# A spectral filter and a gated feed-forward on one core: another order of the opening stage

## Chip, cores and metric

One NeuronCore of a Trainium2 chip. The metric is the device time of one execution in microseconds (us). Engines: TensorE (PE; weight loads are shown as PEld), VectorE (DVE), ScalarE (ACT), GpSimd (POOL) and SyncE, whose queue (SP) issues all transfers of this kernel.

## What is computed

```python
x = A_x                                    # (1, 2048, 640) bf16
xn = layernorm(x)                          # over the 640, eps 1e-5
s = irfft2(rfft2(xn) * (w_r + 1j * w_i))   # over both axes, in fp32, rounded to bf16
g = silu((gelu(xn @ w_gate) * (xn @ w_up)) @ w_down)   # 640 -> 1536 -> 640
return x + s * g
```

## The kernel before

**Tiles.** The 2048 rows are 16 slabs of 128 rows (slab n1 holds the rows n1, n1 + 16, ...). X holds all of them, 640 columns each, and is normalised in place. The feed-forward works on four groups of four slabs, that is 512 rows, as columns of xnT[g] (640 as 5 x 128 partitions, by 512). The 1536 hidden features are 12 tiles t of 128. A piece `ffn_piece(g, t, k, c0, c1)` (lines 782 to 795) is five matmuls over the 5 x 128 of the contraction, with the gate weights (k = 0, PSUM tag psg, evicted by a gelu on ACT to `ge`) or the up weights (k = 1, PSUM tag psu, multiplied by `ge` on DVE into `uT`). Each of the two PSUM tags has two buffers, `ge` has three. The spectral part is done by matmuls with sine tables, which are made on chip from constants of one column (`fwd_consts`, `inv_consts`, `inv_rest`, `ft_v`, lines 283 to 355), and stands between the pieces of the feed-forward later on.

**Order.** The schedule is written by hand: each engine runs its instructions in the order in which the program issues them, and waits in that order. `back` (line 854) is the list of TensorE's steps, `plan[s]` what other work is put behind step s by `put`. Steps 0 to 2 work on slabs 0 and 1 with tiles t = 0, 1, 2, 128 columns at a time (`ffn_slab`). Then come `ffn_part(0, t, 0)` for t = 3 to 7, with 256 columns (slabs 0 and 1), then the second half, `ffn_part(0, t, 1)` for t = 0 to 7 (slabs 2 and 3), and then whole groups of 512 columns.

**The opening.** SP issues the loads in the order of lines 95 to 109: x of slab 0, gate tiles 0 to 2, x of slab 1, up tile 0, up tiles 1 and 2, x of slabs 2 and 3, and the other weights. Per slab, `stats` is two BATCH_NORM_STATS2 of 320 columns and one aggregate on DVE, `root` adds eps on DVE and raises to -0.5 on POOL, `norm` subtracts and multiplies on DVE, and TensorE transposes (`slab_Tparts` in two parts of three and two blocks for slabs 0 and 1, `slab_T` in one for slabs 2 and 3), with a copy out of PSUM. Until slab 0 is there, TensorE runs matmuls on a tile of ones (`warm_pe`, 19 and then 2), whose results are not used. ACT loads its gelu table by a small ACTIVATE at line 215. `root(0, 1)` (line 321) is followed on DVE by the nine operations of `inv_consts`; `root(1, 1)` (line 979) by the five of `inv_rest`. Then, after the last lines below, the loop over `back` runs.

Of the kernel before, what the change touches and what calls it, by code (L numbers as in the profile page):

```python
# [12 lines left out]
ACT = mybir.ActivationFunctionType  # L13
# [19 lines left out]
def kernel(  # L33
# [40 lines left out]
    with tc.manual_schedule():  # L74
        build(nc, locals())


def build(nc, env):
# [5 lines left out]
    def load_x(n0, n, eng=nc.sync):  # L84
        eng.dma_start(out=X[:, n0:n0 + n, :], in_=xv[:, n0:n0 + n, :])

    def load_w(k, t0, t1):
        f0, f1 = t0 * P, t1 * P
        nc.sync.dma_start(out=(Wg, Wu)[k][:, :, f0:f1], in_=(wgv, wuv)[k][:, :, f0:f1])

    def load_gu(t0, t1):
        for k in range(2):
            load_w(k, t0, t1)

    load_x(0, 1)
    load_w(0, 0, 3)
    load_x(1, 1)
    load_w(1, 0, 1)
    load_w(1, 1, 3)
    load_x(2, 2)  # L100
    load_gu(3, 5)
    load_gu(5, 7)
# [63 lines left out]
    def c1(name, dt=FP32):  # L166
        return consts.tile([P, 1], dt, name=name)

    done = set()
    mva = {}  # L170
    rstd = {}
# [7 lines left out]
    def half_stats(n1, k):  # L179
        if k == 0:  # L180
            st_n[n1] = work.tile([P, 2, nc.vector.BN_STATS_DIM], FP32, tag="st", bufs=3, name="st")
        st = st_n[n1]
        nc.vector.bn_stats(out=st[:, k, :], in_=X[:, n1, 320 * k:320 * k + 320])  # L183
        if k == 1:
            g = n1 // 4
            if g not in mva:
                mva[g] = work.tile([P, 4, nc.vector.BN_AGGR_DIM], FP32, tag="mva", bufs=2, name=f"mva{g}")
            nc.vector.bn_aggr(out=mva[g][:, n1 % 4, :], in_=st)

    def stats(n1):  # L190
        for k in range(2):
            half_stats(n1, k)

    def root(n0, n):
        m = mva[n0 // 4][:, n0 % 4:n0 % 4 + n, :]
        ve = work.tile([P, 4], FP32, tag="ve", name="ve")[:, 0:n]
        nc.vector.tensor_scalar(out=ve, in0=m[:, :, 1], scalar1=1e-5, scalar2=None, op0=ALU.add)  # L197
        r = work.tile([P, 4], FP32, tag="rst", bufs=4, name="rst")[:, 0:n]
        nc.gpsimd.tensor_tensor(out=r, in0=ve, in1=mhalf[:, 0:n], op=ALU.pow)  # L199
        rall[n0] = r  # L200
        for k in range(n):
            rstd[n0 + k] = r[:, k:k + 1]

    def norm(n1, c0=0, c1_=D):
        nc.vector.tensor_scalar(out=X[:, n1, c0:c1_], in0=X[:, n1, c0:c1_], scalar1=mva[n1 // 4][:, n1 % 4, 0:1],  # L205
                                scalar2=rstd[n1], op0=ALU.subtract, op1=ALU.mult)
        if c1_ == D:
            done.add(("n", n1))
# [3 lines left out]
    negpi = c1("negpi")  # L212
    nc.vector.memset(negpi, -PI_SAFE)
    warm = c1("warm")
    nc.scalar.activation(out=warm, in_=negpi, func=ACT.Gelu_apprx_tanh)
    b_0, b_1 = c1("b_0"), c1("b_1")
    nc.vector.memset(b_0, 320.0)
    nc.vector.memset(b_1, 0.0)
# [34 lines left out]
    def affine(name, src, a, b):  # L253
        t = c1(name)
        nc.vector.tensor_scalar(out=t, in0=src, scalar1=float(a), scalar2=float(b), op0=ALU.mult, op1=ALU.add)
        return t
# [7 lines left out]
    def fma(name, src, k, add, dt=FP32):  # L264
        t = c1(name, dt)
        nc.vector.scalar_tensor_tensor(out=t, in0=src, scalar=float(k), in1=add, op0=ALU.mult, op1=ALU.add)
        return t
# [8 lines left out]
    def times(name, src, k, by):  # L276
        t = c1(name)
        nc.vector.scalar_tensor_tensor(out=t, in0=src, scalar=k, in1=by, op0=ALU.mult, op1=ALU.mult)
        return t
# [18 lines left out]
    def inv_consts():  # L298
        i_0 = affine("i_0", pf, 4.0, 0.0)
        i_1 = affine("i_1", pf, 4.0, 4.0)  # L300
        i_2 = affine("i_2", pf, 4.0, 2.0)
        o_0 = affine("o_0", pf, 2.0, 320.0)
        o_1 = affine("o_1", pf, 2.0, 2.0)
        o_2 = affine("o_2", pf, 2.0, 321.0)
        o_3 = affine("o_3", pf, 2.0, 1.0)
        ab.extend([(i_0, o_0), (i_1, o_1), (i_2, o_2), (i_2, o_3)])
        kc.append(affine("l_s", s_f, 2.0, 256.0))
        kc.append(affine("hk", h_f, -2.0, 1.0))

    def inv_rest():  # L310
        cq, l_s, hk = kc
        l_k = fma("l_k", h_f, 2.0, l_s)
        l_r = fma("l_r", times("lh", hk, 1.0, hi_f), 1.0, l_k)
        i_r = affine("i_r", l_r, 2.0, 0.0)
        o_r = fma("o_r", l_r, 1.0, cq)
        ab.append((i_r, o_r))
# [1 line left out]
    fwd_consts()  # L318
    vt_iota(0)
    stats(0)  # L320
    root(0, 1)
    inv_consts()

    def tinv_phase(h):
        sl = slice(8 * h, 8 * h + 8)
# [260 lines left out]
    def warm_pe(n):  # L586
        if not warm_bank:
            warm_bank.append(bank(0))
        for _ in range(n):
            nc.tensor.matmul(warm_bank[0][:, 0:256], lhsT=ones[:, 0:P], rhs=ones, start=True, stop=True)  # L590
# [180 lines left out]
    def bank(k):  # L771
        return psA.tile([P, 512], FP32, tag="gu"[k], name="ps" + "gu"[k])
# [55 lines left out]
        for t, k in tk:  # L828
            ffn_piece(0, t, k, j * P, j * P + P)

    GG, REST = ((0, 0), (1, 0)), ((0, 1), (2, 0))

    def run(*items):
        for it in items:
# [2 lines left out]
    PARTS = ((0, 3), (3, 5))  # L837

    def norm_parts(n1):
        for a, b in PARTS:  # L840
            norm(n1, a * P, b * P)

    def slab_Tparts(n1):
        if n1 == 0:
            xnT[0] = xg.tile([P, 5, 512], BF16, tag="xg", name="xnT0")
        for (a, b), ev in zip(PARTS, (nc.scalar.copy, nc.scalar.copy if n1 == 0 else nc.vector.tensor_copy)):
            pt = psB.tile([P, 5, P], BF16, tag="b")
            for c in range(a, b):
                nc.tensor.transpose(out=pt[:, c, :], in_=X[:, n1, c * P:(c + 1) * P], identity=ident)
            ev(out=xnT[0][:, a:b, n1 * P:n1 * P + P], in_=pt[:, a:b, :])  # L850
        done.add(("T", n1))

    NP = 8
    back = [(run, (ffn_slab, 0, GG), (norm_parts, 1), (vt_iota, 1), (ffn_slab, 0, REST), (slab_Tparts, 1),
             (ffn_slab, 0, ((1, 1), (2, 1))),
             (half_stats, 2, 0)),
            (run, (ffn_slab, 1, GG + REST[:1]), (half_stats, 2, 1), (root, 2, 1), (ffn_slab, 1, REST[1:])),
            (run, (ffn_slab, 1, ((1, 1), (2, 1))), (norm, 2), (stats, 3), (root, 3, 1))]
    for h in range(2):
        for t in range(0 if h else 3, NP):  # L860
            back.append((ffn_part, 0, t, h))
# [7 lines left out]
    plan = [[] for _ in back]  # L869

    def put(s, *item):
        plan[s].append(item)

    put(5, norm, 3)
    put(5, slab_T, 2, 1)
    put(6, slab_T, 3, 0)
    for g in range(5):
        put(3 + g, ft_v, g)
        put(8 + g, ft_v, 5 + g)
# [79 lines left out]
    for i, (n0, n) in enumerate(DG):  # L959
        a = vs0 + 7 * i  # L960
# [10 lines left out]
            if (n0 + k) % 2 and 1 < (n0 + k + 3) // 2 < 8:  # L971
                put(min(d + (5 + k if n == 3 else 2), vs0 + 41), load_xt, (n0 + k + 3) // 2)

    warm_pe(19)
    norm_parts(0)
    stats(1)
    slab_Tparts(0)
    warm_pe(2)
    root(1, 1)
    inv_rest()  # L980

    put(5, phase_const)

# [35 lines left out]
```

## Time and profile before

| | |
|---|---|
| median of 3 runs | 201.75 us (201.51 to 202.1) |
| the profiled execution | 201.22 us |
| its span, first to last instruction | 199.4 us |
| TensorE busy | 193.1 us (97%) |
| DVE busy | 131.6 us (66%) |
| ACT busy | 123.1 us (62%) |
| POOL busy | 38.0 us (19%) |
| first matmul that is used (transpose of slab 0) | starts 5.53 us |
| first matmul of the feed-forward | starts 6.59 us |
| second half (slabs 2 and 3) | starts 17.71 us |

Times in the profile are microseconds from the start of the span. A timeline line gives the start, the length, the engine, the source line, the operation, output and inputs with their shapes, how many were merged into the line, and, in brackets, how long the engine had been idle and who released it. Matmuls overlap: the length of a merged line is from the first start to the last end, and five matmuls of 128 columns that take 0.44 us follow the five before them after 0.28 us. Lines on DMA give the size and the time from issue to landing.

### The profile page before, as it was taken

What the parts mean: (1) busy time and instruction counts of PE and PEld (TensorE: products, weight loads), DVE (VectorE), ACT (ScalarE), POOL (GpSimd) and SP (SyncE); (2) the same over time, 40 slices, a digit from 0 to 9 for tenths busy, and PEclk for the clock granted to TensorE, in tenths of its full rate; (3) what the DMA queues carried; (4) which work ended last, traced back from release to release, by engine and by line L of the source; (5) the groups of instructions that cost most, each with busy time, mean ns of one, the idle gap of its engine ahead of it and who ended that gap; (6) DMA issues with size and microseconds to landing.
All of it is one profiled execution on the core that took longest, in us unless ns stands there. A gap on an engine that the chain in (4) does not pass through costs nothing.

```text
span 199.4 us, 4150 instructions
## 1 busy us (share of the span) xinstructions
PE 193.1 (97%) x1534; PEld 118.9 (60%) x1549; DVE 131.6 (66%) x320; ACT 123.1 (62%) x217; POOL 38.0 (19%) x62
## 2 busy tenths in 40 slices
PE   7989999999999999999999999999999999999993
PEld 5778854777555555576633333457765555556772
DVE  7876869999899832223666556423339786878673
ACT  2547657956976677634788687523474747376632
POOL 5427769999030000000000000000000000000000
PEclk9999999999999999999999999999999999999999
DMA  5999999464566647329962022359800416142522
GB/s 176 333 327 337 388 308 186 88 210 173 154 150 158 150 126 278 104 66 298 282 182 98 5 99 102 132 135 292 235 0 35 135 36 194 36 131 46 187 69 66
DMA packets 40325, 32.44 MB, mean 163 GB/s; under 512 B 15088, under 2 KB 38256, under 8 KB 40048
## 3 DMA queue, kind: packets, MB, share of 16 engines
q1 hardware_dynamic: 40304, 32.17, 55.3%
q8 instruction: 12, 0.20, 0.4%
q14 instruction: 9, 0.07, 0.1%
HBM read 19.03 MB, written 7.88 MB: 135 GB/s over the span
## 4 chain that ended last, share of the span: by engine, by line
PE 91%; DVE 4%; DMA 1%; issue 1%; ACT 1%; POOL 1%
PE psu L789 25%; PE psg L789 25%; PE psg L814 13%; PE psu L814 13%; PE pv L706 2%; PE pd L553 2%; PE pu L653 2%; PE pz L543 2%; PE pd L574 2%; PE px L626 2%; DVE st L183 1%; DMA X<-in_A_x_dram 1%; PE pd L557 1%; POOL rst L199 1%; DVE X L205 1%
## 5 line engine op out<-in xcount | busy, mean ns | idle before, releaser
L789 PE MATMUL psu<-xnT,Wu 128*128 128x512 bf16 (+2 forms) x288 | 60.8, 339 | 0.9 <-DVE uT L795 0.3
L789 PE MATMUL psg<-xnT,Wg 128*128 128x512 bf16 (+2 forms) x287 | 60.5, 338 | 0.5 <-issue 0.2
L795 DVE TENSOR_TENSOR uT<-psu,ge 128x512 bf16<-128x512 f32 (+2 forms) x59 | 34.4, 586 | 27.2 <-PE psu L789 21.0
L814 PEld LDWEIGHTS <-uT 128*128 128x128 bf16 x396 | 37.3, 98 | 14.0 <-issue 0.4
L793 ACT ACTIVATE ge<-psg 128x512 bf16<-128x512 f32 (+2 forms) x59 | 30.6, 519 | 22.9 <-PE psg L789 21.1
L789 PEld LDWEIGHTS <-Wu 128*128 128x128 bf16 x295 | 26.9, 98 | 24.7 <-issue 3.2
L789 PEld LDWEIGHTS <-Wg 128*128 128x128 bf16 x295 | 26.6, 98 | 20.6 <-issue 1.6
L814 PE MATMUL psg<-Wd,uT 128*128 128x320 bf16 (+1 forms) x204 | 30.7, 294 | 0.0
L814 PE MATMUL psu<-Wd,uT 128*128 128x320 bf16 (+1 forms) x192 | 28.7, 296 | 0.0
L638 DVE TENSOR_TENSOR X<-xs,W 128x972 bf16<-128x972 bf16 (+2 forms) x22 | 13.3, 648 | 10.2 <-ACT xs L634 9.2
L579 ACT CAST zd<-pd 128x660 bf16<-128x660 f32 x16 | 11.3, 709 | 9.8 <-PE pd L576 6.1
L708 ACT CAST W<-pv 128x640 bf16<-128x640 f32 x16 | 11.1, 696 | 5.0 <-PE pv L706 5.0
L183 DVE BATCH_NORM_STATS2 st<-X 128x6 f32<-128x320 bf16 x32 | 14.0, 477 | 0.3 <-DMA X<-in_A_x_dram 0.3
L731 ACT ACTIVATE W<-pd 128x960 bf16<-128x960 f32 (+2 forms) x14 | 10.1, 780 | 5.6 <-PE pd L557 5.5
L659 ACT CAST X<-pu 128x486 bf16<-128x486 f32 (+4 forms) x22 | 12.3, 558 | 0.3
L634 ACT CAST xs<-px 128x972 bf16<-128x972 f32 (+2 forms) x11 | 10.3, 938 | 2.9 <-PE px L626 2.9
L545 ACT CAST GEN<-pz 128x640 bf16<-128x640 f32 x16 | 11.2, 700 | 1.2 <-PE pz L543 1.2
L823 DVE SCALAR_TENSOR_TENSOR G<-th,psg 128x320 bf16<-128x320 f32 x8 | 3.9, 488 | 12.0 <-ACT th L822 12.0
L737 DVE TENSOR_TENSOR W<-W 128x960 bf16<-128x960 bf16 (+1 forms) x12 | 6.9, 599 | 3.9 <-ACT W L731 3.8
L764 DVE TENSOR_TENSOR Yall<-Yall,G 128x640 bf16<-128x640 bf16 (+3 forms) x19 | 8.3, 435 | 1.6 <-ACT G L819 1.3
L765 DVE TENSOR_TENSOR Yall<-Yall,xt 128x640 bf16<-128x640 bf16 (+3 forms) x19 | 8.3, 439 | 0.7
L199 POOL TENSOR_TENSOR rst<-ve,mhalf 128x1 f32<-128x1 f32 (+1 forms) x7 | 6.0, 854 | 13.8 <-DVE ve L197 13.8
(134 smaller groups left out, 208.3 us busy)
## 6 DMA issues: line engine op xcount, KB each, us to landing
W<-W SPq DMA_DIRECT2D x4, 642.0 KB, 6.0
ZDR<-zd SPq DMA_DIRECT2D x32, 80.2 KB, 2.5
xt<-in_A_x_dram SPq DMA_DIRECT2D x8, 320.0 KB, 3.5
UDR<-X SPq DMA_DIRECT2D x10, 240.8 KB, 2.3
out_dram<-Yall SPq DMA_DIRECT2D x14, 160.0 KB, 2.2
B<-ZDR SPq DMA_DIRECT2D x8, 240.8 KB, 4.3
W<-UDR SPq DMA_DIRECT2D x4, 481.5 KB, 6.8
X<-in_A_x_dram SPq DMA_DIRECT2D x3, 640.0 KB, 6.5
```

Source lines behind the costliest of these rows:

```text
L183: nc.vector.bn_stats(out=st[:, k, :], in_=X[:, n1, 320 * k:320 * k + 320])
L545: nc.scalar.copy(out=Zt[n1], in_=pz)
L579: nc.scalar.copy(out=zd.rearrange("p c (q e) -> p c q e", e=10), in_=pd[:, :, 0:330].rearrange("p c (e q) -> p c q e", q=33))
L634: nc.scalar.copy(out=xs, in_=px[:, :, 0:n * w].rearrange("p k (h l) -> p k h l", l=w))
L638: nc.vector.tensor_tensor(out=pp[-1], in0=xs, in1=WT[:, :, h0:h0 + n, l0:l0 + w], op=ALU.mult)
L659: nc.scalar.copy(out=us[:, :, :, c0:c0 + (w + 1 - m) // 2], in_=pv[:, :, :, m:w:2])
L708: nc.scalar.copy(out=vs, in_=pv)
L731: nc.scalar.activation(out=eo[:, b, :, a0:a1].rearrange("p k a n -> p a k n"), in_=py[b][:, a0:a1], func=ACT.Copy, scale=(2.0 if silu[a0] ...
L789: nc.tensor.matmul(ps, lhsT=WT[:, c, t * P:(t + 1) * P], rhs=xnT[g][:, c, c0:c1_], start=(c == 0), stop=(c == 4))
L793: nc.scalar.activation(out=ges[t], in_=ps, func=ACT.Gelu_apprx_tanh)
L795: nc.vector.tensor_tensor(out=uT[g][:, t, c0:c1_], in0=ps, in1=ges[t], op=ALU.mult)
L814: nc.tensor.matmul(ph, lhsT=uT[g][:, t, j * P:(j + 1) * P], rhs=Wd[:, t, c0:c1_], start=(t == 0), stop=(t == NT - 1))
```

## The change

The changed kernel computes the same. These are its parts:

- **Loads.** Two gate tiles, not three, are loaded ahead of slab 1's x; then up tiles 0 and 1, then the third gate and the third up tile.
- **Root of slab 0.** It is computed on ACT with Abs_reciprocal_sqrt (bias eps) in place of the add on DVE and the power on POOL. The first small ACTIVATE now loads that function's table, and a second one behind the root loads gelu's.
- **Statistics of slab 1.** The first half is issued ahead of the norm of slab 0, the second behind the copy of slab 0's transposes. That copy is made by DVE (three blocks) and ACT (two blocks), where ACT made both.
- **Constants.** `inv_consts` moves from behind slab 0's root to step 5, `inv_rest` from behind slab 1's root to step 6.
- **Order of the pieces.** For slab 0: gate 0, gate 1, up 0, (norm of slab 1), up 1, gate 2, (transposes of slab 1), up 2. For slab 1: the three gate pieces, up 0, up 1, (norm of slab 2), up 2.
- **Statistics of slabs 2 and 3.** Slab 2's are issued whole, with the root, between slabs 0 and 1; slab 3's in halves at steps 3 and 4, the root at step 4. The transposes of slab 2 move from step 5 to step 4. An empty step 2 keeps the numbers of the others.
- **Warm matmuls.** 17 and 4 in place of 19 and 2.

```diff
     load_x(0, 1)
-    load_w(0, 0, 3)
+    load_w(0, 0, 2)
     load_x(1, 1)
-    load_w(1, 0, 1)
-    load_w(1, 1, 3)
+    load_w(1, 0, 2)
+    load_gu(2, 3)
     load_x(2, 2)
...
+    def root_act(n1):
+        rstd[n1] = c1("rst0")
+        nc.scalar.activation(out=rstd[n1], in_=mva[n1 // 4][:, n1 % 4, 1:2], func=ACT.Abs_reciprocal_sqrt, bias=eps)
+        nc.scalar.activation(out=warm, in_=negpi, func=ACT.Gelu_apprx_tanh)
...
-    nc.scalar.activation(out=warm, in_=negpi, func=ACT.Gelu_apprx_tanh)
+    eps = c1("eps")
+    nc.vector.memset(eps, 1e-5)
+    nc.scalar.activation(out=warm, in_=eps, func=ACT.Abs_reciprocal_sqrt)
...
     stats(0)
-    root(0, 1)
-    inv_consts()
+    root_act(0)
+    half_stats(1, 0)
...
-    GG, REST = ((0, 0), (1, 0)), ((0, 1), (2, 0))
+    GG, UU = ((0, 0), (1, 0), (2, 0)), ((0, 1), (1, 1), (2, 1))
...
-        for (a, b), ev in zip(PARTS, (nc.scalar.copy, nc.scalar.copy if n1 == 0 else nc.vector.tensor_copy)):
+        evs = (nc.scalar.copy, nc.vector.tensor_copy)
+        for (a, b), ev in zip(PARTS, evs[::-1] if n1 == 0 else evs):
...
-    back = [(run, (ffn_slab, 0, GG), (norm_parts, 1), (vt_iota, 1), (ffn_slab, 0, REST), (slab_Tparts, 1),
-             (ffn_slab, 0, ((1, 1), (2, 1))),
-             (half_stats, 2, 0)),
-            (run, (ffn_slab, 1, GG + REST[:1]), (half_stats, 2, 1), (root, 2, 1), (ffn_slab, 1, REST[1:])),
-            (run, (ffn_slab, 1, ((1, 1), (2, 1))), (norm, 2), (stats, 3), (root, 3, 1))]
+    back = [(run, (ffn_slab, 0, GG[:2] + UU[:1]), (norm_parts, 1), (vt_iota, 1), (ffn_slab, 0, UU[1:2] + GG[2:]),
+             (slab_Tparts, 1),
+             (ffn_slab, 0, UU[2:]), (stats, 2), (root, 2, 1)),
+            (run, (ffn_slab, 1, GG + UU[:2]), (norm, 2), (ffn_slab, 1, UU[2:]))]
...
+    back.insert(2, (run,))
+    plan.append([])
+    put(3, half_stats, 3, 0)
+    put(4, half_stats, 3, 1)
+    put(4, root, 3, 1)
+    put(4, slab_T, 2, 1)
     put(5, norm, 3)
-    put(5, slab_T, 2, 1)
     put(6, slab_T, 3, 0)
+    put(5, inv_consts)
+    put(6, inv_rest)
...
-    warm_pe(19)
+    warm_pe(17)
     norm_parts(0)
-    stats(1)
     slab_Tparts(0)
-    warm_pe(2)
+    half_stats(1, 1)
+    warm_pe(4)
     root(1, 1)
-    inv_rest()
```

## The prediction

> **What bounds the kernel now.** I read the page's chain of waits first, then the timeline of the first 18 us engine by engine, then the DMA issues one by one, with their time to landing.
>
> ```profile
> span 199.4 us, 4150 instructions
> ...
> PE 91%; DVE 4%; DMA 1%; issue 1%; ACT 1%; POOL 1%
> ```
>
> TensorE is the chain for 91%. Nearly all of the rest lies in the first 15 us, before TensorE runs without a break, and no later piece of the chain is a transfer. So a microsecond lost or won before TensorE's steady stretch reaches the end one to one. The opening chain, on VectorE (DVE) and GpSimd (POOL):
>
> ```profile
> 3.99 0.21 DVE L188 BATCH_NORM_AGGREGATE mva<-st 128x2 f32<-128x12 f32 x1
> 4.24 0.15 DVE L197 TENSOR_SCALAR ve<-mva 128x1 f32<-128x1 f32 x1
> 4.47 0.58 POOL L199 TENSOR_TENSOR rst<-ve,mhalf 128x1 f32<-128x1 f32 x1 [0.59 <-DVE ve L197]
> 5.09 0.64 DVE L205 TENSOR_SCALAR X<-X,mva,rst 128x384 bf16<-128x384 bf16 x2 [0.15 <-POOL rst L199]
> 5.64 0.88 DVE L183 BATCH_NORM_STATS2 st<-X 128x6 f32<-128x320 bf16 x2
> ```
>
> The reader sees slab 0's root take from 4.20 to 5.05 and its norm start at 5.09; only then come the statistics of slab 1. TensorE in the same stretch:
>
> ```profile
> 1.17 4.24 PE L590 MATMUL psg<-GEN 128*128 128x256 bf16 x19 [1.17 <-DVE negpi L213]
> 5.53 0.71 PE L849 MATMUL pt<-ident,X 128*128 128x128 bf16 x5
> 6.03 0.60 PE L590 MATMUL psg<-GEN 128*128 128x256 bf16 x2
> 6.59 0.82 PE L789 MATMUL psg<-xnT,Wg 128*128 128x128 bf16 x10
> ...
> 10.12 0.44 PE L789 MATMUL psu<-xnT,Wu 128*128 128x128 bf16 x5
> 10.88 0.44 PE L789 MATMUL psu<-xnT,Wu 128*128 128x128 bf16 x5 [0.31 <-DVE uT L795]
> ...
> 11.93 0.71 PE L789 MATMUL psu<-xnT,Wu 128*128 128x256 bf16 x5
> ```
>
> A group of five 128-column matmuls costs 0.28 us when groups follow each other (two in 0.56), of 256 columns 0.55. From 6.59 on, TensorE waits 0.11 (second half of slab 0's transpose), 0.33 (slab 1's norm), then three times for a late uT of DVE: 0.48 before 10.88, 0.23 before 11.93, 0.31 before 14.41. These three, 1.01 us, are what less DVE work in the stretch can win at most. From 14.41 to 17.71 there is no wait. The transfers:
>
> ```profile
> Wg<-in_B_w_gate_dram SPq DMA_DIRECT2D x1, 480.0 KB, 3.8
> ...
> X<-in_A_x_dram SPq DMA_DIRECT2D x1, 160.0 KB, 3.7
> ```
>
> The gate tiles, issued at 1.18, land at 4.98; x of slab 1, issued at 1.65, at 5.35, well after slab 0's statistics are done (4.20).
>
> **Root on ScalarE (ACT).** It takes away the DVE add (0.15) and the POOL power (0.58) with their hand-overs. ACT starts 0.03 after 4.20; an ACTIVATE of 128x1 took 0.20 (the warm one at 2.01), so the root is there at 4.45, 0.64 before 5.09. Behind it stand a table reload and a warm ACTIVATE. What a reload costs in mid-stream:
>
> ```profile
> 34.21 0.60 ACT L793 ACTIVATE ge<-psg 128x512 bf16<-128x512 f32 x1 [0.75 <-PE psg L789]
> 34.82 1.28 ACT L335 ACT_TABLE_LOAD   x1
> 36.12 0.20 ACT L335 ACTIVATE warm<-negpi 128x1 f32<-128x1 f32 x1
> ```
>
> From the end at 34.81 to the next start: 1.31. So ACT is free at 4.45 + 1.31 + 0.20 = 5.96, before it has slab 0's second part to copy (6.63 below): cost nothing. The Trainium skill, "ScalarE: Activation LUTs", section "What ACT_TABLE_LOAD costs", puts every switch at about 2.66 us, half of it a drain. By that ACT would be free at 7.31 and the copy 0.7 later, and the sum would be 0.5 us worse; the trace shows no drain in these rows, so the row decides.
>
> **Statistics of slab 1, first half, ahead of norm 0.** This is the step that I price highest. DVE runs its instructions in the order written, so norm 0 and all behind it now wait for slab 1's x. Ahead of that x go 320 instead of 480 KB of gate tiles. Bounds: 160 KB fewer at the 306 to 357 GB/s of 3 to 5 us is 0.46 to 0.54 us, landing 4.85; if the number of packets set the pace (640 either way), 5.35 as now. The packet records have 36 ns for 768 B and 27 ns for 512 B; 640 of them on 16 engines are 0.36 us less, so I take 5.0. The half then runs from 5.02, DVE is free 0.40 later (second half follows 0.40 behind the first at 5.64), and **norm 0 starts at 5.42, not 5.09**: the root's 0.64 is not collected. With the rows' distances: transposes 0.44 later (5.53 - 5.09) at 5.86; the copy 0.53 to 0.6 after that. The three-block part is now DVE's: 0.36, between 0.29 for 256 and 0.48 for 640 columns, done 6.84; ACT's part done 7.01. Four warm matmuls instead of two end just before. The first group starts 6.93 (6.59 now), its fourth matmul at 7.06 (6.87).
>
> **Norm of slab 1.** The copy stands on DVE ahead of the second half of the statistics: 6.76 to 7.24, aggregate 7.48, add 7.66, POOL 0.57 from 7.75 to 8.32 (its root stays there), norm 8.35 against 7.63; its transposes at 8.79 against 8.07, 0.72 late. TensorE has five groups instead of four before them: 0.28 back. Net **+0.44**.
>
> **New order of the groups.** Behind the transposes of slab 1 stands one group (0.28), not two. ACT's copy of its first part starts 0.38 after the transposes and takes 0.48, so slab 1's first group starts at 9.69: a new wait of **0.25**. Three gate groups now stand in a row with two psg buffers: the third waits for the first one's gelu (ends 10.44): **0.25**. DVE does both halves of slab 2's statistics (0.88), aggregate and add ahead of slab 1's first uT, which ends at 11.61 and releases the last up group: **0.33**, in place of the old 0.48.
>
> **Statistics of 3, norm 2, inverse constants.** The old waits of 0.23 and 0.31 go: -0.54, since statistics 3 (two halves of 0.48 beside a uT of 0.42) each fit under 1.09 us of matmuls. But slab 3's root is ready only at 16.3 and norm 3 starts 16.36, so its transposes, after the sixth tile, wait **0.27**. The nine inverse constants (0.06 each apart, 0.54 plus 0.14 for the last) and the five others (about 0.6, with their waits) no longer stand at 4.31 and 6.87, where they ran beside POOL's power: nothing won there. At their new places they hold up the copy of slab 3's transposes (done 18.16, needed 18.2, under the 1.09 us of the seventh tile; without that cover up to 0.4) and one uT, which has over a microsecond. Nothing.
>
> **Loads.** One issue more on SP's queue (0.4 to 0.5 us), which from 5.90 on is held up by a full queue anyway (2.34 us for one issue). By the packet records the finer tiles cost 0.36 us in all; x of slab 2 lands at 8.7 instead of 8.35 and is wanted at 9.98, gate tile 3 at 9.7 and is wanted at 11.9. Nothing.
>
> **Sum.** 0.44 + 0.25 + 0.25 + 0.33 - 0.48 - 0.54 + 0.27 = +0.52: second half's first group at 18.23 where the trace has 17.71. The same adding of rows gives before 17.60, 0.11 too early; an error that both share, so I take +0.63. The profiled execution took 201.22 (span 199.4 and 1.8 around it), 0.3% under the median of 201.75; against it 201.85, against the median **202.4**. Own range by the bounds: x at 4.85 gives +0.5, at 5.35 +1.0; DVE's pause at 10.0 to 10.5, which no row explains (all that uT needs was done at 10.05), may come at another place for 0.3 more, or vanish: 201.9 to 203.0.
>
> **Rivals.** *Full rate comes late.* The warm matmuls stand 0.213 apart (4.24 for 19, two in 0.60 at 6.03), twice the 0.11 that 256 columns take later: the rate doubles at about 6.4, 5.2 us after the first matmul, with only 0.12 idle before. Now 17 warm ones end at 5.0 and the transposes come at 5.86: a pause of 0.86. If the pause makes it start over, at 10 to 11 us, twelve groups cost 0.26 more each, 3.1; the waits above hide over half: +1.3 on mine, **203.7**. Against: 0.86 of it is short. The Trainium skill, "TensorE: Matmul & The Clock Gate", part 1, has the clock released after a busy, free-running window of about 3.4 us; the 5.2 us here agree, and by that the next chance would be near 9.8. *x is early.* If it lands by 4.5, norm 0 starts by 4.9, the first group at 6.5, but the chain behind is as above: +0.15, **201.9**. Against: 640 KB by 4.1 do not fit the rates. *The three uT waits go and nothing replaces them.* x lands by 4.2, norm 0 at 4.6, slab 1's norm stays under the fifth group, DVE, which has 1.3 us of constants less before 8 us, is never late: -1.01, -0.11 for the second half, +0.4 of the new waits: **201.0**. It decides if no wait of TensorE between 8 and 15 us exceeds 0.2. For: the stretch does hold less DVE work; against: landing and copy order.
>
> **Chances.** Mine 0.48 (0.38 of it over 0.3%), late rate 0.20, early x 0.08, waits gone 0.24. A difference under 0.3% (0.6 us, the spread of the three runs) could not be told from none: slower 0.58, same 0.20, faster 0.22. Range 201.0 to 203.7.
>
> **What would show it.** Right: slab 1's first half-statistics start at the landing near 5.0, norm 0 behind it near 5.4, slab 1's norm past 8.2. Wrong: norm 0 before 5.0; 128-column matmuls 0.107 apart after 7 us; an ACT copy that waits for the table; TensorE unbroken from 8.

## The result and the profile after

| | median | runs | span of the profiled execution |
|---|---|---|---|
| before | 201.52 us | 201.36 to 202.1 (6) | 199.4 us (execution 201.22) |
| after | 204.14 us | 203.25 to 204.63 (6) | 202.8 us (execution 204.57) |

The ratio is 1.0121, 95% interval 1.0092 to 1.0149: the change makes the kernel 1.2% slower, and the time lies above the predicted range. The profiled execution is 3.35 us longer than that of before. The first part of the page and the chain of waits of after:

```profile
span 202.8 us, 4168 instructions
...
PE 195.5 (96%) x1549; PEld 119.9 (59%) x1549; DVE 133.8 (66%) x321; ACT 124.3 (61%) x219; POOL 37.6 (19%) x61
...
PE 90%; DVE 4%; DMA 2%; ACT 1%; issue 1%; SPq 0%; POOL 0%; DVEq 0%
```

TensorE is still the chain, and of the 3.4 us by which the span grew, it is busy in up to 2.4 (195.5 against 193.1, where 15 matmul records of before are missing), though it computes the same. So some of its work ran at a lower rate, and the rest are waits. The timeline of after, VectorE and ScalarE, from the end of slab 0's statistics:

```profile
4.26 0.29 ACT L206 ACTIVATE rst<-mva,eps 128x1 f32<-128x1 f32 x1 [2.05 <-DVE mva L188]
4.57 1.28 ACT L207 ACT_TABLE_LOAD   x1
4.91 0.50 DVE L183 BATCH_NORM_STATS2 st<-X 128x6 f32<-128x320 bf16 x1 [0.69 <-DMA X<-in_A_x_dram]
5.32 0.62 DVE L210 TENSOR_SCALAR X<-X,mva,rst 128x384 bf16<-128x384 bf16 x2
...
6.49 0.37 ACT L858 COPY xnT<-pt 128x256 bf16<-128x256 bf16 x1 [0.42 <-PE pt L857]
```

The root is ready at 4.55 instead of 5.05, but VectorE stands for 0.69 us at the half statistics of slab 1 until that x has landed, and the norm of slab 0 starts at 5.32, later than before (5.09). ScalarE's copy at 6.49 waited for TensorE and not for the table. TensorE in after (each line: start, length of the merged stretch, number of matmuls):

```profile
1.17 3.81 PE L597 MATMUL psg<-GEN 128*128 128x256 bf16 x17 [1.17 <-DVE eps L221]
5.74 0.71 PE L857 MATMUL pt<-ident,X 128*128 128x128 bf16 x5 [0.76 <-DVE X L210]
6.25 1.06 PE L597 MATMUL psg<-GEN 128*128 128x256 bf16 x4
7.10 1.27 PE L796 MATMUL psg<-xnT,Wg 128*128 128x128 bf16 x10
8.17 1.27 PE L796 MATMUL psu<-xnT,Wu 128*128 128x128 bf16 x10
...
10.56 1.24 PE L796 MATMUL psg<-xnT,Wg 128*128 128x128 bf16 x15
...
18.13 0.45 PE L538 MATMUL pt<-ident,X 128*128 128x128 bf16 x5 [0.51 <-DVE X L210]
...
22.38 0.71 PE L796 MATMUL psu<-xnT,Wu 128*128 128x256 bf16 x5 [1.07 <-DVE uT L802]
```

Three things are to be seen. The ten matmuls from 7.10 take until 8.17, 0.107 us each, and the ten behind them too, while those of a group in the fifteen from 10.56 follow at 0.056: the rate doubles at about 9.3, where before it did so at about 6.5. The transposes of slab 3 wait for that slab's norm. And an up group at 22.38 waits 1.07 us for a `uT` of VectorE, in a stretch where before had no wait at all. VectorE ahead of that wait, in the same trace:

```profile
18.54 0.15 DVE L273 SCALAR_TENSOR_TENSOR ph_t<-e,hi 128x1 f32<-128x1 f32 x1
...
19.34 0.76 DVE L273 SCALAR_TENSOR_TENSOR l_k<-pb,l_s 128x1 f32<-128x1 f32 x1
20.02 0.15 DVE L285 SCALAR_TENSOR_TENSOR lh<-hk,pb 128x1 f32<-128x1 f32 x1
20.20 1.08 DVE L273 SCALAR_TENSOR_TENSOR l_r<-lh,l_k 128x1 f32<-128x1 f32 x1
21.31 0.15 DVE L262 TENSOR_SCALAR i_r<-l_r 128x1 f32<-128x1 f32 x1
21.38 0.61 DVE L273 SCALAR_TENSOR_TENSOR o_r<-l_r,cq 128x1 f32<-128x1 f32 x1
21.92 0.41 DVE L802 TENSOR_TENSOR uT<-psu,ge 128x256 bf16<-128x256 f32 x1
```

and GpSimd beside it:

```profile
18.89 2.38 POOL L333 TENSOR_SCALAR GEN<-GEN,u,ph_t 128x1024 int32<-128x1024 int32 x2 [1.30 <-DVE ph_t L273]
21.24 0.75 POOL L369 TENSOR_SCALAR GEN<-GEN 128x660 f32<-128x660 f32 x1
```

These are the five operations of `inv_rest`, 128 values each. They run from 19.34 to 21.99, 2.65 us. Three of them take 0.61 to 1.08 us, where the same form took 0.15 at 18.54. The two merged GpSimd operations end at 20.09 and 21.27, the third at 21.99; the three slow ones end at 20.09, 21.28 and 21.99. Each ended when the GpSimd operation beside it ended. Of the other two, `i_r` reads one tensor; `lh` reads two, began 0.08 before the end of the first GpSimd operation, and took 0.15.

**Where the 3.35 us arose.** The gelus of the feed-forward are 59 in every kernel, so the start of the n-th can be held against that of the profiled execution of before. The lag in us, here and for all the experiments below:

| gelu (its start in before) | 12th (18.46) | 15th (21.74) | 34th (79.28) | 36th (100.79) |
|---|---|---|---|---|
| after | 1.79 | 3.26 | 3.26 | 3.36 |
| e1_one_input | 0.29 | 0.29 | 0.34 | 1.53 |
| e2_warm20 | 0.68 | 2.14 | 2.14 | 2.68 |
| e3_before_warm15 | 1.07 | 1.07 | 1.10 | 1.11 |
| e4_half_behind | 0.52 | 1.26 | 1.25 | 2.59 |
| e5_before_loads | 0.05 | 0.05 | 0.10 | 0.10 |
| e6_one_input_loads | 0.99 | 0.99 | 1.03 | 1.03 |
| e7_all_three | 0.06 | 0.06 | 0.08 | 0.51 |
| e8_before_rest | -0.39 | 1.08 | 1.17 | 1.17 |
| f1_rest_one_input | 0.08 | 0.08 | 0.08 | 0.08 |
| f2_root_act | 0.18 | 0.18 | 0.24 | 0.54 |
| f3_both | -0.29 | -0.29 | -0.23 | -0.23 |

In after, 1.79 us are lost before the second half of the first group begins, 1.47 around `inv_rest`, nothing for the next 57 us, and 0.10 near 80 us.

### The profile page after: what moved, and what is told of

It reads as the page before. It is cut to its first block, busy times and chain, and to the rows that moved or that the text cites. A ratio compares the mean times of both kernels' runs of the same rounds, so it can differ in the third digit from the quotient of the medians.

```text
span 202.8 us, 4168 instructions
## 1 busy us (share of the span) xinstructions
PE 195.5 (96%) x1549; PEld 119.9 (59%) x1549; DVE 133.8 (66%) x321; ACT 124.3 (61%) x219; POOL 37.6 (19%) x61
## 4 chain that ended last, share of the span: by engine, by line
PE 90%; DVE 4%; DMA 2%; ACT 1%; issue 1%; SPq 0%; POOL 0%; DVEq 0%
PE psu L796 25%; PE psg L796 25%; PE psg L821 13%; PE psu L821 13%; PE pv L713 2%; PE pd L560 2%; PE pu L660 2%; PE pz L550 2%; PE pd L581 2%; PE px L633 2%; DMA X<-in_A_x_dram 2%; PE pd L564 1%; DVE uT L802 1%; DVE st L183 1%; DVE l_r L273 1%
## 5 line engine op out<-in xcount | busy, mean ns | idle before, releaser
L796 PE MATMUL psu<-xnT,Wu 128*128 128x512 bf16 (+2 forms) x295 | 61.9, 343 | 1.3 <-DVE uT L802 1.2
L796 PE MATMUL psg<-xnT,Wg 128*128 128x512 bf16 (+2 forms) x295 | 61.9, 343 | 0.2
L796 PEld LDWEIGHTS <-Wu 128*128 128x128 bf16 x295 | 27.4, 100 | 25.5 <-issue 4.0
L796 PEld LDWEIGHTS <-Wg 128*128 128x128 bf16 x295 | 27.2, 100 | 20.8 <-issue 1.8
L199 POOL TENSOR_TENSOR rst<-ve,mhalf 128x1 f32<-128x1 f32 (+1 forms) x6 | 5.4, 904 | 16.7 <-DVE ve L197 16.7
```

Of the source, the lines that this page charges most:

```text
L796: nc.tensor.matmul(ps, lhsT=WT[:, c, t * P:(t + 1) * P], rhs=xnT[g][:, c, c0:c1_], start=(c == 0), stop=(c == 4))
```

## The experiments

Each is compared with runs of before on the same chip: 201.32 us median for e1 to e4, 201.31 for e5 to e8, 201.42 for f1 to f3.

**e1_one_input: the same constants without a second tensor input.** After, with three operations of `inv_rest` written with one tensor input and two column operands (two columns, 1.0 and 2.0, are set in the opening):

```diff
-        l_k = fma("l_k", h_f, 2.0, l_s)
-        l_r = fma("l_r", times("lh", hk, 1.0, hi_f), 1.0, l_k)
+        l_k = one_in("l_k", h_f, l_two, l_s)
+        l_r = one_in("l_r", hk, hi_f, l_k)
         i_r = affine("i_r", l_r, 2.0, 0.0)
-        o_r = fma("o_r", l_r, 1.0, cq)
+        o_r = one_in("o_r", l_r, l_one, cq)
...
+    def one_in(name, src, a, b):
+        t = c1(name)
+        nc.vector.tensor_scalar(out=t, in0=src, scalar1=a, scalar2=b, op0=ALU.mult, op1=ALU.add)
+        return t
```

> The five late constants at step 6 are made by instructions with one tensor input (and column operands), four instead of five; nothing else moves but two early memsets. Theory: in the changed kernel the three long ones (0.76, 1.08, 0.61 us against 0.15 alone) are VectorE instructions with two tensor inputs that stand still while GpSimd's L333 runs (18.89 to 21.27); so here each takes about 0.15, the four together under 0.7 instead of 2.65 us, TensorE's waits of 1.23 us at 21.15 and 0.24 at 23.47 go, and the time falls by 1.2 to 1.5 us, to about 202.8. Rival: something else holds VectorE there (its instructions arrive late, the fetch at 18.69); then the four are as long and the time is 204.1. Beside it: VectorE's unexplained pause of 0.47 us ahead of uT at 15.69 (0.42 at 10.53 before) stands at the 64th VectorE record in both kernels, and behind a single half of statistics in both. Two memsets more: if the position makes it, the pause moves to the half of statistics of slab 3 ahead of that uT; if the single half makes it, it stays at the uT.

Measured: 203.07 us (202.68 to 204.17, 4 runs), ratio 1.0097 (1.0064 to 1.0129). GpSimd and VectorE in its timeline:

```profile
17.38 2.38 POOL L341 TENSOR_SCALAR GEN<-GEN,u,ph_t 128x1024 int32<-128x1024 int32 x2 [1.28 <-DVE ph_t L276]
17.84 0.26 DVE L293 TENSOR_SCALAR l_k<-pb,l_two,l_s 128x1 f32<-128x1 f32 x1
18.13 0.27 DVE L293 TENSOR_SCALAR l_r<-hk,pb,l_k 128x1 f32<-128x1 f32 x1
...
18.51 0.27 DVE L293 TENSOR_SCALAR o_r<-l_r,l_one,cq 128x1 f32<-128x1 f32 x1
```

The GpSimd operation is the same 2.38 us, and the four of `inv_rest` run inside it, in 0.94 us. TensorE's wait of 1.07 us is gone, and the lag does not move between the 12th and the 15th gelu. So the 1.47 us are what `inv_rest` cost by meeting GpSimd. The median fell by 1.07 only; the profiled execution (202.73) lost 1.2 us elsewhere. ScalarE and TensorE near 80 us, same kernel:

```profile
83.07 0.71 ACT L594 CAST zd<-pd 128x660 bf16<-128x660 f32 x1 [2.85 <-DMA ZDR<-zd]
84.43 0.42 PE L589 MATMUL pd<-FT,GEN 128*128 128x132 bf16 x4 [1.02 <-ACT GEN L560]
```

ScalarE waits there for a store. Before waits for the same store for 1.61 us at 81.49, which TensorE does not feel; here it is 2.85, and it does.

**e2_warm20: a shorter pause of TensorE in the opening.** After, with 20 warm matmuls.

```diff
-    warm_pe(17)
+    warm_pe(20)
```

> Only 20 warm matmuls instead of 17: TensorE's pause ahead of slab 0's transposes shrinks from 0.76 to about 0.1 us. Theory: the pause spoils the stretch after which TensorE gets its full rate; without it the 128-column matmuls stand 0.056 apart from about 6 to 6.6 us on, as before, not from 9.3, and the time falls by 1.0 to 1.4 us, to about 203.0. Rival: the rate does not depend on this pause (the start is late for the late x alone): the 0.107 lasts to 9.3 and the time is 204.1 within 0.4.

Measured: 203.85 us (203.07 to 203.86, 4 runs), ratio 1.0114 (1.0093 to 1.0135). TensorE:

```profile
5.85 0.54 PE L857 MATMUL pt<-ident,X 128*128 128x128 bf16 x5 [0.23 <-DVE X L210]
...
6.67 0.74 PE L796 MATMUL psg<-xnT,Wg 128*128 128x128 bf16 x10
```

The pause is 0.23 us, the rate doubles at 5.5, and the first ten matmuls take 0.74 us, not 1.27. At the 12th gelu this execution is 1.11 us ahead of after's (0.68 against 1.79), and it then loses the same 1.46 at `inv_rest`. The median hardly moves, though (203.85 against 204.14, where 203.0 was expected); near 80 us it loses 0.54, where after lost 0.10. So late full rate is what this profiled execution of after lost, and not what every execution of it loses.

**e3_before_warm15: a pause put into before.**

```diff
-    warm_pe(19)
+    warm_pe(15)
```

> The kernel before with 15 warm matmuls instead of 19, nothing else: a pause of about 0.95 us ahead of the transposes at 5.53, which stay where they are. Theory of the pause: the full rate comes some 2.9 to 3.4 us later and the time rises by 0.8 to 1.4 us, to 202.3 to 202.9. Rival (only the length of the work counts, a short pause does not): 201.5 within 0.2.

Measured: 201.70 us (201.18 to 202.45, 10 runs), ratio 1.0021 (1.0005 to 1.0037). TensorE in its profiled execution, which took 202.34:

```profile
5.48 0.71 PE L849 MATMUL pt<-ident,X 128*128 128x128 bf16 x5 [0.93 <-DVE X L205]
...
6.54 1.23 PE L789 MATMUL psg<-xnT,Wg 128*128 128x128 bf16 x10
```

With 0.93 us of pause the rate doubles at 9.9 and the lag is 1.07, all of it by the fourth gelu, 5 us behind the pause. Five of its ten runs lie at 201.18 to 201.46 like before, and five at 201.94 to 202.45, 0.9 us more on average; of before's 14 runs beside them none is above 201.76, and of its 62 runs beside the other kernels 7 are at 201.94 or above. So with a pause of this length about half of the executions are late. That full rate is what they lost is shown for the profiled one alone.

A pause is not enough by itself, though. In the profiled executions of e1 (first line) and e6 (second) it is 0.89 and 1.59 us, and the transposes behind it run at full rate, 0.54 us for five against 0.71 in after and in e3:

```profile
5.87 0.54 PE L865 MATMUL pt<-ident,X 128*128 128x128 bf16 x5 [0.89 <-DVE X L210]
6.57 0.54 PE L865 MATMUL pt<-ident,X 128*128 128x128 bf16 x5 [1.59 <-DVE X L210]
```

The clock records of the traces have the step to full rate at 5.31 in e1 and 5.08 in e6, only 0.33 and 0.10 us into their pauses, which both begin at 4.98. In after and e3 it comes at 9.32 and 9.90, behind the whole pause, and in the nine other profiles, whose pauses are 0.27 us or less, between 5.09 and 6.98. So what seems to count is where the pause lies against the moment of the step, and not its length alone; no run was made to test this.

**e4_half_behind: the half statistics of slab 1 behind the norm of slab 0.** After with

```diff
     root_act(0)
-    half_stats(1, 0)
...
     norm_parts(0)
+    half_stats(1, 0)
     slab_Tparts(0)
```

> The changed kernel with the first half of slab 1's statistics behind the norm of slab 0 instead of ahead of it. Theory: norm 0 then waits for the root alone and starts near 4.6 instead of 5.32, the transposes near 5.05, with no pause behind 17 warm matmuls (end 4.98); the full rate comes on time and the first group of the feed-forward starts near 6.4 instead of 7.1; the time falls by 1.3 to 2.0 us, to 202.1 to 202.8, what is left over 201.5 being the late constants. Rival: slab 1's x is not what norm 0 waited for, or the copies and slab 1's own chain set the pace anyway: less than 0.5 us.

Measured: 202.94 us (202.0 to 203.78, 5 runs), ratio 1.0075 (1.0042 to 1.0108). Its timeline:

```profile
4.57 0.64 DVE L210 TENSOR_SCALAR X<-X,mva,rst 128x384 bf16<-128x384 bf16 x2 [0.36 <-ACT rst L206]
5.00 0.71 PE L856 MATMUL pt<-ident,X 128*128 128x128 bf16 x5
5.13 0.49 DVE L183 BATCH_NORM_STATS2 st<-X 128x6 f32<-128x320 bf16 x1
```

Norm 0 follows the root, TensorE has no pause (the line at 5.00 names no wait), and the first gate group starts at 6.36 instead of 7.10. Norm 0 starts 0.52 earlier than in before (5.09): this is the root's gain, and the half statistics in front of the norm had taken it back. It hardly goes further: the first gelu is 0.05 ahead of before's. The lag grows by 0.74 at `inv_rest`, not by 1.47, because here `l_r` took 0.16 us beside GpSimd, and all five 1.93 in place of 2.65. Near 80 us this execution lost 1.34; the median is a little above the expected 202.1 to 202.8.

**e5_before_loads: the new order of the loads in before.** The first hunk of the change alone.

```diff
-    load_w(0, 0, 3)
+    load_w(0, 0, 2)
     load_x(1, 1)
-    load_w(1, 0, 1)
-    load_w(1, 1, 3)
+    load_w(1, 0, 2)
+    load_gu(2, 3)
```

> The kernel before with the new order of the first loads alone. Theory: the finer tiles make the transfers of the first 30 us later (in the changed kernel x of slabs 12 to 15 lands at 31.6 instead of 29.1), SP's queue, which issues in order, is later by as much, and near 80 us ScalarE waits over 2.5 instead of 1.6 us for a store of ZDR; TensorE, within 0.3 us of before until then, loses about 1 us there: 202.0 to 202.8. Rival: the early lag is caught up by SP's queue: 201.3 within 0.3.

Measured: 201.32 us (201.19 to 201.97, 10 runs), ratio 0.9992 (0.9976 to 1.0009). The finer loads cost nothing here; that they slow all transfers, as I thought after e1 to e4, fell.

**e6_one_input_loads: e1 with before's loads** (the edit of e1, and the lines of e5 the other way).

> The changed kernel with one-input late constants (as in e1) and with the first loads of before. Theory: without the finer loads the loss near 80 us, 1.24 us in e1, goes; x of slab 1 lands at 5.35 and norm 0 starts at 5.76, 0.4 later than in e1, so 0.4 more is lost at the start: 201.8 to 202.5, by when the full rate comes; ScalarE's wait for ZDR near 80 us is under 2 us. Rival: the loss near 80 us has nothing to do with the loads: 203.1 or more.

Measured: 203.01 us (202.27 to 203.38, 6 runs), ratio 1.0072 (1.0047 to 1.0096), above the expected 201.8 to 202.5; the profiled execution is the fastest of the six. With three gate tiles ahead of it, slab 1's x lands later, and norm 0 with it:

```profile
5.74 0.49 DVE L183 BATCH_NORM_STATS2 st<-X 128x6 f32<-128x320 bf16 x1 [1.55 <-DMA X<-in_A_x_dram]
6.15 0.62 DVE L210 TENSOR_SCALAR X<-X,mva,rst 128x384 bf16<-128x384 bf16 x2
```

That is 0.70 behind e1's 5.04 and 5.45, and the lag at the 12th gelu is 0.70 above e1's: once the half statistics stand ahead of the norm, a late x is paid in full. In this execution nothing was lost near 80 us, though the constants stand as in e1, so their order alone does not bring that loss. Where the five slower runs lost their time is not known.

**e7_all_three: one-input constants, before's loads, half statistics behind norm 0** (the edits of e6 and of e4).

> The changed kernel with three parts taken back: one-input late constants, the first loads of before, and the first half of slab 1's statistics behind norm 0. What stays: root of slab 0 on ScalarE, the new order of the groups and statistics. Theory: the three (and the pause of TensorE that the second of them made) are all of the loss: norm 0 starts near 4.6, TensorE's first group near 6.4, the time is 201.0 to 201.7, no slower than before. Rival: the new order of copies, groups and statistics costs as such (the waits of 0.25, 0.25, 0.33 and 0.27 us that the prediction counts): 202.0 to 202.4.

Measured: 201.63 us (201.35 to 202.21, 10 runs), ratio 1.0012 (0.9997 to 1.0027), with a lag of 0.06 to 0.08 until 80 us. Nearly all of the loss is undone, and what stays of the change (root on ScalarE, new order of the pieces, statistics and constants at their new steps) wins nothing.

**e8_before_rest: `inv_rest` alone moved, in before.**

```diff
     put(6, slab_T, 3, 0)
+    put(6, inv_rest)
...
     root(1, 1)
-    inv_rest()
```

> The kernel before with the five late constants moved to step 6, nothing else. Theory: behind the copy of slab 3's transposes (17.65) they meet GpSimd's L333 of the changed kernel (here 16.27 to 18.65) and the two-tensor ones stand until it has ended: 18.7 to 19 instead of 18.3 for the last, uT of the seventh tile 0.7 to 1.3 us late, TensorE waits at the second tile of the second half; the time rises by 0.2 to 1.0 us. Rival: GpSimd does not hold VectorE; the five take 0.7 us and stay under the matmuls: 201.3 within 0.2.

Measured: 202.50 us (202.38 to 203.51, 10 runs), ratio 1.0066 (1.0048 to 1.0083). GpSimd, VectorE and TensorE:

```profile
15.89 2.37 POOL L326 TENSOR_SCALAR GEN<-GEN,u,ph_t 128x1024 int32<-128x1024 int32 x2 [1.70 <-DVE ph_t L266]
...
17.18 0.15 DVE L266 SCALAR_TENSOR_TENSOR l_k<-pb,l_s 128x1 f32<-128x1 f32 x1
17.26 1.01 DVE L278 SCALAR_TENSOR_TENSOR lh<-hk,pb 128x1 f32<-128x1 f32 x1
18.23 0.74 POOL L362 TENSOR_SCALAR GEN<-GEN 128x660 f32<-128x660 f32 x1
18.31 0.68 DVE L266 SCALAR_TENSOR_TENSOR l_r<-lh,l_k 128x1 f32<-128x1 f32 x1
...
20.21 0.71 PE L789 MATMUL psu<-xnT,Wu 128*128 128x256 bf16 x5 [1.07 <-DVE uT L795]
```

Two moved lines of the change cost before 1.19 us (202.50 - 201.31) by themselves. The lag shows 1.47 between the 12th and the 15th gelu, as in after; the 0.39 by which the kernel was ahead until then is the good side of the move. With it TensorE waits once for a `uT` between 10 and 15 us, 0.64 ahead of 11.85, where before waits three times, 1.02 together; a pause of VectorE, described in the last section, falls on another `uT` there.

**f1_rest_one_input: the same move with one-input operations** (the edits of e8 and e1; the two columns are set by GpSimd).

> The kernel before with inv_rest behind the transposes of slab 3 (as in e8_before_rest), and with l_k, l_r and o_r written as operations with one tensor input and two column operands. In e8 TensorE was 0.38 us ahead of before by the first gelus of slab 1 and 1.08 behind after inv_rest. If the contention of two-input VectorE operations with GpSimd's 2.4 us operation is all that inv_rest costs there, the lag stays near -0.4 through slab 1 and the time is 200.8 to 201.1 us against 201.31 of before, faster by about 0.2%. If inv_rest's mere place in VectorE's program is what costs (the uT behind it), the lag rises by about 0.6 to 1.0 and the time is 201.9 to 202.5. The three operations should take 0.2 to 0.3 us each, not 0.68 to 1.01.

Measured: 201.21 us (200.96 to 202.23, 12 runs), ratio 0.9989 (0.9974 to 1.0005).

```profile
17.65 0.26 DVE L286 TENSOR_SCALAR l_k<-pb,l_two,l_s 128x1 f32<-128x1 f32 x1
17.95 0.27 DVE L286 TENSOR_SCALAR l_r<-hk,pb,l_k 128x1 f32<-128x1 f32 x1
```

The place in VectorE's program is the same as in e8, and the lag stays at 0.08 through `inv_rest`. So the second tensor input beside GpSimd costs, and not the place. The time missed the expected 200.8 to 201.1, since the 0.39 of e8 is not there: slab 1's statistics waited for x until 6.01 in this execution (5.57 in e8).

**f2_root_act: slab 0's root on ScalarE, alone, in before.**

```diff
-    root(0, 1)
+    root_act(0)
     inv_consts()
```

> The kernel before with slab 0's root on ScalarE alone (loads, order and constants as before, inv_consts still behind the root). My step for the root: 4.20 to about 4.55, so norm 0 starts where inv_consts, which VectorE has ahead of it, ends: about 4.9 instead of 5.09 and TensorE's first group about 0.2 earlier; the table reload hides. Time 201.0 to 201.4 us, the same within 0.3%. Rival: ScalarE's reload of 1.3 us delays its copies of slab 0's transposes or its DMA work: then its first copy is late and the time is over 201.8. Second question: whether the late landing of x of slabs 12 to 15 (31.6 us and more in all kernels with the change, 29.1 in before) comes with the root; if so it is over 31 here, else below 30.

Measured: 201.61 us (201.24 to 202.08, 12 runs), ratio 1.0011 (1.0 to 1.0021). Norm 0 starts at 4.62 (before 5.09), and the first gelu is only 0.14 earlier; slab 1's x, landing at 5.80 in this execution, then holds up the rest, and by the 12th gelu the lag is +0.18. So the root alone is worth nothing here.

**f3_both: f1 and f2 together.**

> Both together: inv_rest moved with one-input operations, and slab 0's root on ScalarE, all else as in before. If the two gains are separate, TensorE is some 0.4 to 0.6 us ahead of before at the second gelu of slab 1 and the time is 200.6 to 201.0 us against 201.31. If the root gains nothing because norm 0 then waits for inv_consts, it equals f1_rest_one_input within 0.1. If the waits come back later (near 80 us, where ScalarE waits for a store), it is 201.2 or more.

Measured: 201.13 us (200.87 to 202.0, 12 runs), ratio 0.9991 (0.9978 to 1.0003), lag -0.29 at the 12th and 15th gelu. Its median is the lowest of all, but the interval holds 1, so it can't be told from before. Between 10 and 15 us one wait of its TensorE is left, for a `uT`, ahead of 11.94.

## Why the prediction was wrong

**The step that failed: constants at "Nothing".** The prediction priced `inv_rest` at about 0.6 us under a `uT` with "over a microsecond" of room. It took 2.65 us, and 1.47 us reached the end (after 1.79 to 3.26; e8 the same; 0 in e1, f1 and f3). I asked what the operations hold up on VectorE, and not what runs on GpSimd beside them. The rows were there, in before:

```profile
7.03 0.57 POOL L199 TENSOR_TENSOR rst<-ve,mhalf 128x1 f32<-128x1 f32 x1 [1.98 <-DVE ve L197]
7.12 0.16 DVE L266 SCALAR_TENSOR_TENSOR l_r<-lh,l_k 128x1 f32<-128x1 f32 x1
...
16.27 2.38 POOL L326 TENSOR_SCALAR GEN<-GEN,u,ph_t 128x1024 int32<-128x1024 int32 x2 [1.62 <-DVE ph_t L266]
```

At their old place the operations ran beside GpSimd's power and were not held (`l_r` 0.16, `o_r` 0.15). At the new one they meet 2.38 us of another GpSimd operation, which waits for the `ph_t` of step 5 in both kernels. The power works on one value per partition and this one on 1024 at a time; whether that makes the difference, no run shows. The Trainium skill, "SBUF — State Buffer", section "Who interferes with whom", says that a VectorE instruction with two SBUF inputs contends with a GpSimd instruction that reads SBUF, and that one with at most one such input does not, outside the modes that use two ports. The runs at step 6 agree on both: 0.76, 1.08 and 0.61 us against 0.26, 0.27 and 0.27, and a `uT` beside GpSimd, which has one input in PSUM, keeps its 0.41 (18.70 in e1). The same page of the Trainium skill, section "SBUF: two separate sides", says too that whichever of the two starts first has the shared ports for the whole instruction and the other is blocked; the ends at 20.09, 21.28 and 21.99 agree, and the last section has operations that do not.

**The rival that came true as well.** Full rate late was priced at +1.3 on the forecast, with a chance of 0.20. In the profiled execution it cost 1.11 (after less e2 at the 12th gelu). The mechanism and the size were about right, and the chance was probably too low: "against: 0.86 of it is short" was no argument, since in e3 0.93 us of pause is enough in about half of the executions. But neither does a pause always do it (e1, e6), so in a single execution it is luck. The stretches at full rate in the clock records are 191.15, 194.56 or 197.97 us long, in steps of 3.41. One such step ahead of the late 9.32 (after) and 9.90 (e3) are 5.91 and 6.49, just behind pauses that ended at 5.74 and 5.48; this is worked out, not tested. The Trainium skill, "TensorE: Matmul & The Clock Gate", part 1, has the window free-running, so that its place varies from run to run; the steps at 5.08 to 6.98, e3's two clusters 0.9 us apart and after's spread of 203.25 to 204.63 fit that.

**The pause of VectorE.** The prediction allowed 0.3 us for a pause that no row explained. It lies at the same count of VectorE's records in every kernel (below). In after this is a `uT` ahead of slab 3's root, so the transposes at 18.13 start 0.67 later than TensorE was free (16.92 + 0.54), where "slab 3's norm late" had 0.27. In e1, where the pause falls elsewhere, the transposes start 0.26 later than TensorE was free, and the 12th gelu is 0.39 earlier than in e2.

**What was right.** Slab 1's x landed at 4.91 (predicted 5.0), norm 0 started at 5.32 (5.42), the transposes at 5.74 (5.86), and ScalarE's reload took 1.28 and held up nothing. The 2.66 us of the Trainium skill, "ScalarE: Activation LUTs", section "What ACT_TABLE_LOAD costs", do not show here either: the next ACTIVATE starts at 5.87, 1.31 behind the root. That the half statistics take back what the root gains for norm 0 is shown by e4. The loads cost nothing (e5). The chain from there to the second half was forecast at +0.52 and is +0.29 in e1, where neither late full rate nor VectorE's pause disturbs it: the sum of small waits was too high by 0.23. With VectorE's pause it is 0.68, near the +0.63 of the forecast, but that is luck, since 0.39 of it was not in the sum.

So the 3.36 us of the profiled execution are: 0.29 order and half statistics, 0.39 VectorE's pause, 1.11 late full rate, 1.47 `inv_rest` beside GpSimd, 0.10 near 80 us. The first, the second and the fourth, 2.15, should come in every execution, the third in some; the lowest of the six runs, 203.25, is 1.9 above before's lowest. The fourth is shown by several kernels; the first three are read from single executions of e1, e2 and after, and not from a count over many.

**Open.** The stage near 80 us, where ScalarE waits for a store, took between 0 and 1.34 us more from one profiled execution to the next (after 0.10, e1 1.19, e4 1.34, e6 and f1 0). What makes that store late was not settled; e5 was to show that the loads do, and lost nothing there.

## What to carry to other kernels

A small VectorE operation that is moved is priced by what runs beside it at its new place. Here, with two tensors read from SBUF and GpSimd at work on 1024 or 660 values per partition, most such operations of one value per partition took 0.61 to 1.08 us; written with one tensor and column operands they took 0.26 to 0.28. Statistics or any work that waits for a transfer should not stand ahead of work that is ready on the same engine, since the transfer's landing then sets the start of both. A gap of 0.8 to 0.9 us in the warm-up of TensorE cost about 1 us behind it in some executions and nothing in others, so a single profile does not price it.

## What the hardware showed that was not expected

**VectorE pauses at one place of its program.** In the profiled executions of all 13 kernels, the 64th record of VectorE (waits on semaphores counted) starts 0.44 to 0.49 us after the 63rd, whatever it is. Before, where the 64th is a `uT` and TensorE waits for it:

```profile
10.53 0.29 DVE L795 TENSOR_TENSOR uT<-psu,ge 128x128 bf16<-128x128 f32 x1 [0.56 <-PE psg L789]
```

The wait of this `uT` was over at 10.05 (the 63rd record). In e1, with two memsets more in the opening, the 64th is a half of slab 3's statistics, and it is that one which starts late, 0.45 behind its `uT` where after has 0.34 (14.18 to 14.52):

```profile
13.10 0.42 DVE L810 TENSOR_TENSOR uT<-psu,ge 128x256 bf16<-128x256 f32 x1 [0.62 <-PE psu L804]
13.55 0.49 DVE L183 BATCH_NORM_STATS2 st<-X 128x6 f32<-128x320 bf16 x1
```

In after a `uT` at the same step (15.69) started 0.49 behind its semaphore; here (14.19) it started 0.07 behind. So an instruction more or less in the opening moves the pause from one chain to another, to a place where most of it is covered. That it is the fetching of instructions is a guess; no run shows it.

**A two-input operation can slip through.** In after, e2, e4 and e8, `l_k`, `lh`, `l_r` and `o_r` met these GpSimd operations 16 times. Eleven were held, ten of them to within 0.01 us of the end of a GpSimd operation. The other of the eleven, `o_r` in e8, took 0.73 from 19.09 and ended long before the GpSimd operation of 2.44 us beside it (19.06). Five took 0.15 to 0.16: `lh` three times, across the change from one GpSimd operation to the next, `l_k` in e8, 0.11 us into a GpSimd operation, and `l_r` in e4, 0.12 into one. How early it starts does not decide: in after `l_r` started 0.12 into one as well and was held. What does is open.

**GpSimd can be the one that waits.** Later in after GpSimd makes columns of 16 values, 0.37 us each. Beside VectorE's two-input operations on 512 to 1536 values the same ones last up to 1.88 us, while the VectorE operations take what they take alone (0.68 us for the third line):

```profile
40.14 0.37 POOL L385 TENSOR_SCALAR vg<-kr,n1x,phs 128x16 int32<-128x16 int32 x1
43.55 1.88 POOL L385 TENSOR_SCALAR vg<-kr,n1x,phs 128x16 int32<-128x16 int32 x1
44.66 0.68 DVE L476 TENSOR_TENSOR GEN<-X 128x1024 bf16<-128x1024 bf16 x1
```

So the price falls on the one or the other; that the second input is what holds GpSimd here was not tested.
